# Expert products in three fp16 passes instead of three float32r passes, with scale factors from sums of squares and a new order

## The chip, the cores and the metric

The kernel runs on one core of one Trainium2 chip. The core has TensorE (PE, matrix products into PSUM), VectorE (DVE), ScalarE (ACT), GpSimd (POOL) and SyncE (SP, which here issues the transfers); they run side by side and meet in semaphores. The metric is the time of one execution in device microseconds. Three executions of the kernel before took 581.51 us in the median (581.0 to 586.58).

## The reference, cut to what matters

Causal attention with a memory term over 4 batches, 8 heads, 576 positions and 64 dimensions gives 2304 rows of 512 numbers; these rows go through two dense products with a pointwise function between them, and it is these two that the change rewrites.

```python
scores = where(causal, -1e9, q @ k.T / sqrt(64)); local = softmax(scores) @ v
mem_out = (phi(q) @ M_prev) / (phi(q) @ z_prev + 1e-6)          # phi(x) = x + 1 for x > 0, else exp(x)
x = (g * mem_out + (1 - g) * local)  as (2304, 512)             # g = sigmoid(beta), one per head
h = x @ w_in            # 512 x 2048
out = (h * cos(h)) @ w_out   # 2048 x 512
```

## The kernel before, in words

The 2304 rows are cut into nine chunks of 256: chunk 0 holds the first 64 rows of each batch, chunks 1 and 2 the rest of batch 0, and so on to chunks 7 and 8 of batch 3. The attention of a batch must be done before its chunks can start, so the program is a pipeline: while chunks of one batch are multiplied, the heads of the next batch are computed. The jobs are listed in `prm["jobs"]`: batch 0 in two halves, then one batch each.

A **chunk** begins in `emit_xT`: TensorE turns its rows (L886), ScalarE writes a high part `xh` (L897) and VectorE the rest `xl` (L373). Then come eight **units** of 256 hidden columns each. A unit's first half is `unit1` (PE L914, into `u`): for chunks 1 to 8, 24 matmuls of 256 columns, that is for each of two blocks of 128 hidden columns four blocks of the contraction in three terms (high by high, high by low, low by high) on float32r tiles. `hidden` then makes h cos(h): ScalarE rounds `u` to whole turns (L937), VectorE subtracts (L939), ScalarE takes the sine (L941), VectorE multiplies by `u` (L943); the product is split once more into `gh` (a copy, L363 on ScalarE or L365 on VectorE) and `gl` (a subtraction, L373). The second half is `unit2` (PE L958): 12 matmuls per unit (2 row blocks, 2 blocks of hidden columns, 3 terms), each of 512 columns, into `acc`. `live` holds two units back, so the second half of a unit is issued about two units after its first half. `finish` scales `acc` and stores it. Chunk 0 uses unsplit float32 weights (`weight_val`).

The **weights** come as 64-bit numbers. `load_w` turns a piece of 128 by 512 into float32 in four steps (POOL L476, ACT L479, DVE L481, L486); after chunk 0 has used a piece, `split_w` writes its high part (ACT L504) and its low part (DVE L511), 32 pieces in all.

**Attention heads** go through scores (PE L540), a running minimum (DVE L551), exponentials (ACT L558), a split of the probabilities into two fp16 parts (L363 or L365 for the high one, DVE L570 for the rest), a transposing transfer, and the product with the values (PE L712 in fp16, L703 in float32 for batch 0's first heads), which VectorE adds to the rows (L723). `values` scales the values by a power of two (L627) and splits them into fp16 parts (L365 copy, L373 subtraction).

What sets the **order**: nothing is reordered on the chip except weight loads on TensorE. `Plan.order` runs a list scheduler over all operations with estimated costs (`dve`, `act`, `pool`, `mm`), chooses an engine where an operation allows several (`gl_on` = VectorE or GpSimd, `gh_on`, `hi_on`), and emits the instructions of each engine in the order found. The entries `bdve` and `bact` are added to an operation's finish on VectorE and ScalarE when engines are compared. So the numbers in `prm` decide both order and engine.

Of the kernel before, what the change touches and what calls it, by code (L numbers as in the profile page):

```python
# [292 lines left out]
def kernel(  # L293
# [170 lines left out]
    def load_w(key, src, prio):  # L464
# [24 lines left out]
        w_ready[key] = Pp({"DVE": dve(512)}, end, prio, r=[st, t])  # L489

    def split_w(key, prio, used):
        if len(w_split) >= prm["wide"] and wide:
            ph = pl = wide.pop(0)
        else:
            ph, pl = [(places or last).pop(0) for part in range(2)]

        def high(e):
            if ph == pl:
                both = sb.tile([128, 1024], F32R, tag=ph, name=f"{ph}_both")
                wh[key], wl[key] = both[:, 0:512], both[:, 512:1024]  # L500
            else:
                wh[key] = sb.tile([128, 512], F32R, tag=ph, name=f"{ph}_high")
            if e == "ACT":
                nc.scalar.copy(out=wh[key], in_=wv[key])  # L504
            else:
                eng[e].tensor_scalar(out=wh[key], in0=wv[key], scalar1=1.0, scalar2=1.0, op0=ALU.mult, op1=ALU.mult)
# [665 lines left out]
```

## Time and profile before

| | |
|---|---|
| median of three runs | 581.51 us |
| the profiled execution's span, first to last instruction | 578.5 us |
| median minus span | 3.0 us |
| TensorE busy | 567.5 us (98%) |
| VectorE busy | 402.3 us (70%) |
| ScalarE busy | 407.2 us (70%) |
| GpSimd busy | 160.1 us (28%) |

The profiled execution has no time of its own beside its span; its 578.5 us and what lies around it (3.0 us, if it is a median one) make the 581.5. A busy share is a mean over the whole span. The kernel has two halves: up to about 464 us attention and expert products run together and three engines are loaded; after that only expert products are left. Matmuls are pipelined, so a busy TensorE need not stream without gaps; what one matmul costs in a stream is the distance from start to start, not its duration. On VectorE and ScalarE too an instruction starts some 0.08 us before the record of the one ahead ends.

### The profile page before, as it was taken

The numbers are of one execution on the slowest core, as the hardware profiler recorded it, in microseconds if no ns is written. First come the engines' busy times: TensorE is split into PE (matmuls) and PEld (weight loads), VectorE is DVE, ScalarE is ACT, GpSimd is POOL, SyncE is SP. The second block draws the span as 40 slices with busy tenths as digits, with TensorE's granted clock in tenths as the row PEclk, the third lists the DMA queues.
The fourth block names the chain that finished last, engine by engine and source line by source line (L and its number), as shares of the span: only waits on it lengthen the run. The fifth ranks groups of instructions, "written<-read, shape, count | busy, mean of one in ns | idle before, by whom it ended". The sixth has DMA issues, their size and how long they took to land.

```text
span 578.5 us, 12276 instructions
## 1 busy us (share of the span) xinstructions
PE 567.5 (98%) x4453; PEld 468.6 (81%) x4453; DVE 402.3 (70%) x1292; ACT 407.2 (70%) x872; POOL 160.1 (28%) x159
## 2 busy tenths in 40 slices
PE   8899999999999999999999999999999999999997
PEld 5677657688888788788977988888879999989995
DVE  4999788989989899889758855868698421321320
ACT  4997788898898897769657946968788532433432
POOL 2232330145225213115140311441213112222112
PEclk9999999999999999999999999999999999999999
DMA  8877773696644985485509810727056100000101
GB/s 277 286 228 236 241 231 98 122 200 139 140 97 99 182 160 114 92 168 143 81 0 191 168 31 1 164 76 150 1 103 125 31 1 19 19 0 1 38 0 37
DMA packets 113165, 64.96 MB, mean 112 GB/s; under 512 B 95952, under 2 KB 101584, under 8 KB 113104
## 3 DMA queue, kind: packets, MB, share of 16 engines
q1 hardware_dynamic: 113104, 64.18, 46.7%
q8 instruction: 35, 0.57, 0.4%
q14 instruction: 26, 0.21, 0.1%
HBM read 36.37 MB, written 4.72 MB: 71 GB/s over the span
## 4 chain that ended last, share of the span: by engine, by line
PE 81%; ACT 7%; DMA 5%; DVE 3%; issue 2%; SPq 1%; POOL 0%; ACTq 0%; POOLq 0%; DVEq 0%
PE u L914 32%; PE acc L958 31%; PE S L540 7%; PE pv L712 5%; DMA t<-p 2%; PE pv L703 2%; PE mm L669 2%; ACT s L558 2%; PE mm L886 1%; DMA ws<-in_w_in 1%; DVE p L570 1%; DMA q<-in_qk 1%; SPq L379 1%; ACT p L363 1%; ACT x L689 1%
## 5 line engine op out<-in xcount | busy, mean ns | idle before, releaser
L373 POOL TENSOR_TENSOR gl<-w,gh 128x512 fp32r<-128x512 f32 x64 | 84.7, 1325 | 249.7 <-ACT gh L363 175.2
L914 PE MATMUL u<-xh,weight_high 128*128 128x256 f32 x416 | 119.4, 287 | 1.0 <-DVE w L943 1.0
L914 PE MATMUL u<-xl,weight_high 128*128 128x256 f32 x416 | 115.9, 279 | 0.0
L914 PE MATMUL u<-xh,weight_low 128*128 128x256 f32 x416 | 115.7, 278 | 0.0
L939 DVE SCALAR_TENSOR_TENSOR w<-w,u 128x512 f32<-128x512 int32 x72 | 49.1, 684 | 84.7 <-ACT w L937 68.3
L958 PE MATMUL acc<-weight_high,gh 128*128 128x512 f32 x240 | 97.8, 407 | 0.0
L958 PE MATMUL acc<-weight_low,gh 128*128 128x512 f32 x240 | 94.4, 393 | 0.0
L958 PE MATMUL acc<-weight_high,gl 128*128 128x512 f32 x240 | 94.1, 392 | 0.0
L570 DVE SCALAR_TENSOR_TENSOR p<-s,p 128x64 f16<-128x64 f32 (+1 forms) x224 | 83.1, 414 | 6.2 <-ACT p L363 5.6
L914 PEld LDWEIGHTS u<-xh,weight_high 128*128 128x128 f32 x416 | 78.3, 188 | 6.5 <-issue 2.5
L558 ACT ACTIVATE s<-s,nb 128x448 f32<-128x448 f32 (+3 forms) x128 | 77.6, 610 | 5.9 <-DVE nb L551 5.6
L914 PEld LDWEIGHTS u<-xl,weight_high 128*128 128x128 f32 x416 | 78.3, 188 | 1.4
L914 PEld LDWEIGHTS u<-xh,weight_low 128*128 128x128 f32 x416 | 78.5, 189 | 0.0
L937 ACT ACTIVATE w<-u 128x512 int32<-128x512 f32 x72 | 42.4, 592 | 47.3 <-PE u L914 28.0
L363 ACT ACTIVATE gh<-w 128x512 fp32r<-128x512 f32 x56 | 35.2, 628 | 49.0 <-PE acc L958 40.6
L551 DVE CUSTOM_DVE_ANT_0 s<-S,mask 128x320 f32<-128x320 f32 (+3 forms) x128 | 65.5, 532 | 4.1 <-PE S L540 3.8
L943 DVE TENSOR_TENSOR w<-w,u 128x512 f32<-128x512 f32 x64 | 43.5, 683 | 22.4 <-ACT w L941 22.3
L540 PE MATMUL S<-stq 64*128 64x320 f32 (+4 forms) x320 | 55.6, 455 | 0.0
L941 ACT ACTIVATE w<-w 128x512 f32<-128x512 f32 x72 | 45.0, 629 | 14.8 <-DVE w L939 14.0
L958 PEld LDWEIGHTS acc<-weight_high,gh 128*128 128x128 f32 x240 | 45.1, 188 | 11.2 <-issue 2.7
L958 PEld LDWEIGHTS acc<-weight_low,gh 128*128 128x128 f32 x240 | 45.1, 188 | 10.1
L958 PEld LDWEIGHTS acc<-weight_high,gl 128*128 128x128 f32 x240 | 45.2, 188 | 7.5
(123 smaller groups left out, 1037.0 us busy)
## 6 DMA issues: line engine op xcount, KB each, us to landing
ws<-in_w_in SPq DMA_DIRECT2D x16, 512.0 KB, 5.4
ws<-in_w_out SPq DMA_DIRECT2D x16, 512.0 KB, 4.2
stq<-in_qkp SPq DMA_DIRECT2D x12, 544.0 KB, 4.2
stv<-in_vk SPq DMA_DIRECT2D x16, 320.0 KB, 3.3
out<-w SPq DMA_DIRECT2D x16, 256.0 KB, 2.2
t<-p SPq DMA_TRANSPOSE x112, 3.2
mz<-in_mzp SPq DMA_DIRECT2D x20, 66.0 KB, 2.6
stq<-in_qkp SPq DMA_DIRECT2D x4, 288.0 KB, 3.6
```

Source lines behind the costliest of these rows:

```text
L363: nc.scalar.activation(out=out, in_=in_, func=ACTF.Copy, scale=scale)
L373: lambda e: eng[e].tensor_tensor(out=out, in0=in0, in1=in1, op=ALU.subtract), prio, port=kw.pop('port', True), **kw)
L540: nc.tensor.matmul(out=sv.ap[:, c:c + n], lhsT=pair.ap[p, qs], rhs=pair.ap[p, k0:k0 + n], start=True, stop=True)
L551: return P.op({"DVE": dve(n) + 10}, lambda e: nc.vector.tensor_tensor_reduce(out=st.ap[:, k0:k0 + n], in0=sv.ap[:, c:c + n], in1=mk, scale ...
L558: return P.op({"ACT": act(W, False, 2)}, lambda e: nc.scalar.activation(out=st.ap[:, 0:W], in_=st.ap[:, 0:W], func=ACTF.Exp, scale=-1.0, b ...
L570: Pp({"DVE": dve(n)}, lambda e, c=c, n=n, to=to: nc.vector.scalar_tensor_tensor(out=pt.ap[:, to:to + n], in0=sa[:, c:c + n], scalar=PSCALE ...
L914: nc.tensor.matmul(out=u.ap[:, f, :], lhsT=a[:, cs:cs + 128], rhs=x, start=(n == 0), stop=(n == len(terms) - 1))
L937: P.op({"ACT": act(512)}, lambda e: nc.scalar.activation(out=wi, in_=u.ap, func=ACTF.Copy, bias=0.25), ep, r=[u], w=[w])
L939: P.op({"DVE": dve(512)}, lambda e: nc.vector.scalar_tensor_tensor(out=wv, in0=wi, scalar=0.25, in1=u.ap, op0=ALU.subtract, op1=ALU.subtra ...
L941: P.op({"ACT": act(512, False)}, lambda e: nc.scalar.activation(out=wv, in_=wv, func=ACTF.Sin, scale=-TWO_PI_BELOW), ep, w=[w], table="sin")
L943: P.op({"DVE": dve(512)}, lambda e: nc.vector.tensor_tensor(out=wv if split else views[0], in0=wv, in1=u.ap, op=ALU.mult), ep, r=[u], w=[w ...
L958: nc.tensor.matmul(out=acc[b].ap, lhsT=a, rhs=w, start=(i == 0 and f == 0 and n == 0), stop=(2 * i + f == NF - 1 and n == len(terms) - 1))
```

## The change

Expert products of chunks 1 to 8 take fp16 tiles: `xh`, `xl`, `gh`, `gl` and the split weights become fp16, and a piece of weights has both parts in one tile. So that the parts fit the range of fp16, each is scaled by a power of two: `squares` sums the squares of a piece of weights or of a chunk's rows (ScalarE or VectorE, with a running sum), `powers` adds the sums over partitions with a small matmul and makes a scale from the exponent bits in five small VectorE instructions, and `factors` makes common factors of the eight weight groups once. The scales enter as operands that hold one number per partition: in the copies and subtractions that split, in the rounding and subtraction of `hidden`, in the product with `u` and in `finish`. `xh` and `xl` have two buffers instead of one. Chunk 0 stays as it was.

Lines move by 84 at the end; of the names used here: L914 becomes L985, L958 L1039, L712 L773, L939 L1012, L943 L1016, L373 (subtractions) L381, L365 L373, L627 L688, L511 L568, L570 L631, L551 L612.

```diff
-    group("xh", 1, [128, KD, 256], F32R)
-    group("xl", 1, [128, KD, 256], F32R)
+    group("xh", 2, [128, KD, 256], F16)
+    group("xl", 2, [128, KD, 256], F16)
-    group("gh", 2, [128, 2, 256], F32R)
-    group("gl", 2, [128, 2, 256], F32R)
+    group("gh", 2, [128, 2, 256], F16)
+    group("gl", 2, [128, 2, 256], F16)
...
+        w_norm[key] = squares(prio, wv, key, norms[:, o, j, n:n + 1], after=[w_ready[key]])
+
+    def squares(prio, src, key, to, **kw):
+        def go(e):
+            x = src[key]
...
+                if e == "ACT":
+                    nc.scalar.activation(out=junk[e], in_=x, func=ACTF.Square, accum_out=to)
+                else:
+                    nc.vector.tensor_tensor_reduce(out=junk[e], in0=x, in1=x, scale=1.0, scalar=0.0, op0=ALU.mult,
+                                                   op1=ALU.add, accum_out=to)
...
+    def powers(prio, src, n, q, sc, r=(), a=(), after=()):
+        bank = P.buf("mm")
+        P.op({"PE": 60}, lambda e: nc.tensor.matmul(out=bank.ap[:, 0:n], lhsT=ones.to_broadcast([128, 128]), rhs=src,
+                                                    start=True, stop=True), ...
+        def go(e):
+            nc.vector.tensor_reduce(out=q, in_=bank.ap[:, 0:n], axis=mybir.AxisListType.X, op=ALU.add)
+            nc.vector.tensor_scalar(out=q, in0=q, scalar1=2.0**-100, scalar2=1.0, op0=ALU.max, op1=ALU.mult)
+            nc.vector.tensor_scalar(out=q.bitcast(I32), in0=q.bitcast(I32), scalar1=1, scalar2=0x7F800000, ...)
+            nc.vector.tensor_scalar(out=sc.bitcast(I32), in0=q.bitcast(I32), scalar1=0x7F800000, scalar2=None, ...)
+            nc.vector.tensor_scalar(out=sc, in0=sc, scalar1=2.0**-51, scalar2=None, op0=ALU.mult)
+        return P.op({"DVE": 450}, go, prio, r=[bank], a=a)
...
+                nc.scalar.activation(out=wh[key], in_=wv[key], func=ACTF.Copy, scale=s)
...
-            eng[e].tensor_tensor(out=wl[key], in0=wv[key], in1=wh[key].bitcast(F32), op=ALU.subtract)
+            eng[e].scalar_tensor_tensor(out=wl[key], in0=wv[key], scalar=s, in1=wh[key], op0=ALU.mult, op1=ALU.subtract)
...
+        if len(w_scale) == 8 and not w_fac:
+            w_fac.append(factors(prio))
...
+            P.op({"ACT": act(512, extra=1)}, lambda e: nc.scalar.activation(
+                out=wi, in_=u.ap, func=ACTF.Copy, scale=d, bias=0.25), ep, r=[u, cs], w=[w])
+            P.op({"DVE": dve(512)}, lambda e: nc.vector.scalar_tensor_tensor(
+                out=wv, in0=u.ap, scalar=d, in1=wi, op0=ALU.mult, op1=ALU.subtract), ep, r=[u, cs], w=[w])
+            P.op({"ACT": act(512, False, 1)}, lambda e: nc.scalar.activation(
+                out=wv, in_=wv, func=ACTF.Sin, scale=TWO_PI_BELOW, bias=quarter), ep, w=[w], table="sin", ...)
+            P.op({"DVE": dve(512)}, lambda e: nc.vector.scalar_tensor_tensor(
+                out=wv, in0=wv, scalar=ej, in1=u.ap, op0=ALU.mult, op1=ALU.mult), ep, r=[u], w=[w], after=w_fac)
...
-    "bdve": 1205.026,
-    "bact": 739.67,
+    "bdve": 60.616892,
+    "bact": -403.610341,
+    "sq_on": ('ACT', 'DVE'),
```

Some twenty numbers of `prm` change in all, among them the start `t0` of the chunks and the priorities `xt`, `u2`, `wdt`, `late`; the jobs and the engines that an operation may choose from stay.

Where instructions move. The first place is **GpSimd** behind the last of the weight pieces (`wt`), where the heads of batch 1 and chunk 1 begin: `stv` and `v` are values of heads, `gl` the low part of a unit's hidden numbers. Before:

```order
L476 TENSOR_SCALAR wt_139<-ws_137 128x512
L627 TENSOR_SCALAR stv_67<-stv_67,vs_108 128x640
L365 TENSOR_SCALAR v_72<-stv_67 128x640
L373 TENSOR_TENSOR v_72<-stv_67,v_72 128x640
L627 TENSOR_SCALAR stv_68<-stv_68,vs_109 128x640
L365 TENSOR_SCALAR v_73<-stv_68 128x640
L373 TENSOR_TENSOR v_73<-stv_68,v_73 128x640
L373 TENSOR_TENSOR gl_106<-w_102,gh_104 128x512
L373 TENSOR_TENSOR gl_107<-w_103,gh_105 128x512
```

and now, to the end of GpSimd's work:

```order
L485 TENSOR_SCALAR wt_154<-ws_152 128x512
L688 TENSOR_SCALAR stv_74<-stv_74,vs_123 128x640
L373 TENSOR_SCALAR v_79<-stv_74 128x640
L688 TENSOR_SCALAR stv_75<-stv_75,vs_124 128x640
L688 TENSOR_SCALAR stv_75<-stv_75,vs_125 128x640
L373 TENSOR_SCALAR v_80<-stv_75 128x640
L381 TENSOR_TENSOR v_80<-stv_75,v_80 128x640
```

Before, GpSimd makes all 64 low parts `gl` and all 16 value splits; now it makes 3 of the 64 and 4 of the 16, and the others stand on VectorE.

The second place is **VectorE** around the first two units of chunk 1 (`w` is a unit's working tile, `s`, `S` and `p` belong to the heads). Before:

```order
L939 SCALAR_TENSOR_TENSOR w_103<-w_103,u_129 128x512
L570 SCALAR_TENSOR_TENSOR p_92<-s_83,p_92 128x384
L676 SCALAR_TENSOR_TENSOR r_124<-mm_133,gate 128x4
L943 TENSOR_TENSOR w_102<-w_102,u_128 128x512
L679 RECIPROCAL r_124<-r_124 128x4
L723 SCALAR_TENSOR_TENSOR x_97<-pv_132,sm_121,x_97 128x64
L685 TENSOR_TENSOR x_96<-mm_133,r_124 128x128
L685 TENSOR_TENSOR x_97<-mm_133,r_124 128x128
L570 SCALAR_TENSOR_TENSOR p_90<-s_87,p_90 128x512
L943 TENSOR_TENSOR w_103<-w_103,u_129 128x512
```

and now:

```order
L1016 SCALAR_TENSOR_TENSOR w_111<-w_111,wfac,u_143 128x512
L662 RECIPROCAL sm_133<-sm_133 128x2
L373 TENSOR_SCALAR gh_113<-w_111 128x512
L784 SCALAR_TENSOR_TENSOR x_104<-pv_147,sm_133,x_104 128x64
L784 SCALAR_TENSOR_TENSOR x_103<-pv_147,sm_133,x_103 128x64
L381 TENSOR_TENSOR gl_115<-w_111,gh_113 128x512
L1012 SCALAR_TENSOR_TENSOR w_112<-u_144,cs_117,w_112 128x512
L631 SCALAR_TENSOR_TENSOR p_99<-s_90,p_99 128x384
```

A unit now takes three or four VectorE instructions of 512 columns instead of two (in eight of the 64 units three), between the same work for the heads.

The third place is **VectorE** where chunk 1's rows are split (`xl`). Before:

```order
L570 SCALAR_TENSOR_TENSOR p_93<-s_82,p_93 128x384
L511 TENSOR_TENSOR weight_low<-weight_val,weight_high 128x512
L373 TENSOR_TENSOR xl_101<-mm_133,xh_100 128x4x128
L511 TENSOR_TENSOR wide_both<-weight_val,wide_both 128x512
L511 TENSOR_TENSOR weight_low<-weight_val,weight_high 128x512
```

and now (`wq`, `wsc`, `wfac` and `cs` hold sums and scales):

```order
L528 TENSOR_REDUCE cs_117<-mm_148 128x1
L529 TENSOR_SCALAR cs_117<-cs_117 128x1
L530 TENSOR_SCALAR cs_117<-cs_117 128x1
L532 TENSOR_SCALAR cs_117<-cs_117 128x1
L534 TENSOR_SCALAR cs_117<-cs_117 128x1
L568 SCALAR_TENSOR_TENSOR weight_both<-weight_val,wsc,weight_both 128x512
L942 TENSOR_SCALAR cs_117<-wfac,cs_117 128x5
L373 TENSOR_SCALAR p_97<-s_94 128x576
L568 SCALAR_TENSOR_TENSOR weight_both<-weight_val,wsc,weight_both 128x512
```

Each chunk and each of the eight weight groups has such a chain of small instructions, in which each reads what the one ahead wrote, and the scale stands ahead of what it scales.

## Rows read from the trace of the kernel before

**Rows 1.** The page, busy time and share of each engine.

```profile
PE 567.5 (98%) x4453; PEld 468.6 (81%) x4453; DVE 402.3 (70%) x1292; ACT 407.2 (70%) x872; POOL 160.1 (28%) x159
```

**Rows 2.** The chain in order of time: start us, us, what, records.

```profile
161.08 1.12 PE S L540 x8
...
221.96 1.12 PE pv L712 x38
...
500.66 5.47 PE u L914 x48
...
560.91 13.77 PE acc L958 x60
```

**Rows 3.** Busy time by stretch: PE, PEld, DVE, ACT, POOL, granted clock, DMA.

```profile
0.00:97.00 97.00, 91.33 (x527) 65.03 (x527) 80.70 (x259) 77.48 (x192) 27.82 (x49) 1.00 0.74 238
97.00:160.00 63.00, 62.93 (x527) 48.87 (x527) 57.05 (x177) 56.04 (x112) 21.54 (x18) 1.00 0.69 138
160.00:235.00 75.00, 74.50 (x678) 61.65 (x679) 66.87 (x245) 67.42 (x157) 23.23 (x20) 1.00 0.67 138
235.00:297.00 62.00, 62.00 (x584) 52.17 (x581) 47.19 (x158) 41.94 (x89) 16.62 (x14) 1.00 0.50 99
297.00:579.00 282.00, 276.70 (x2145) 240.93 (x2143) 150.52 (x455) 164.33 (x324) 70.94 (x58) 1.00 0.28 59
```

**Rows 4.** Timeline of ScalarE at the last unit of chunk 3.

```profile
297.00 0.60 ACT L937 ACTIVATE w<-u 128x512 int32<-128x512 f32 x1 [1.46 <-POOL gl L373]
```

**Rows 5.** VectorE's groups by shape: busy us, mean ns, idle before.

```profile
L570 DVE SCALAR_TENSOR_TENSOR p<-s,p 128x512 f16<-128x512 f32 x32 | 25.7, 804 | 0.0
L551 DVE CUSTOM_DVE_ANT_0 s<-S,mask 128x512 f32<-128x512 f32 x32 | 20.9, 683 | 3.8 <-PE S L540 3.8
L551 DVE CUSTOM_DVE_ANT_0 s<-S,mask 128x192 f32<-128x192 f32 x32 | 11.1, 348 | 0.3 <-PE mm L587 0.3
L551 DVE CUSTOM_DVE_ANT_0 s<-S,mask,nb 128x64 f32<-128x64 f32 x32 | 8.9, 277 | 3.6 <-PE S L540 3.3
L624 DVE TENSOR_SCALAR vs<-gate,vs 128x2 f32<-128x2 f32 x16 | 8.7, 546 | 0.2
L365 DVE TENSOR_SCALAR gh<-w 128x512 fp32r<-128x512 f32 x8 | 3.4, 420 | 0.2
```

**Rows 6.** Timeline of VectorE, full instructions back to back.

```profile
149.72 0.68 DVE L570 SCALAR_TENSOR_TENSOR p<-s,p 128x512 f16<-128x512 f32 x1
150.32 0.45 DVE L365 TENSOR_SCALAR p<-s 128x576 f16<-128x576 f32 x1
...
154.18 0.68 DVE L943 TENSOR_TENSOR w<-w,u 128x512 f32<-128x512 f32 x1
154.78 0.68 DVE L939 SCALAR_TENSOR_TENSOR w<-w,u 128x512 f32<-128x512 int32 x1
```

**Rows 7.** Timeline of VectorE, small instructions on the gates.

```profile
9.91 0.17 DVE L427 TENSOR_SCALAR gate<-gate 128x8 f32<-128x8 f32 x1
10.11 0.20 DVE L428 RECIPROCAL gate<-gate 128x8 f32<-128x8 f32 x1
10.35 0.17 DVE L429 TENSOR_SCALAR gate<-gate 128x8 f32<-128x8 f32 x1
```

**Rows 8.** GpSimd's costliest group by shape.

```profile
L373 POOL TENSOR_TENSOR gl<-w,gh 128x512 fp32r<-128x512 f32 x64 | 84.7, 1325 | 249.7 <-ACT gh L363 175.2 <-issue 20.4 <-DVE gh L365 18.3
```

**Rows 9.** Timeline of GpSimd and of VectorE, a small instruction beside `gl`.

```profile
151.15 1.68 POOL L373 TENSOR_TENSOR gl<-w,gh 128x512 fp32r<-128x512 f32 x1 [5.49 <-ACT gh L363]
...
151.81 1.05 DVE L598 TENSOR_SCALAR sm<-sm,vs 128x2 f32<-128x2 f32 x1
...
153.66 0.20 DVE L598 TENSOR_SCALAR sm<-sm,vs 128x2 f32<-128x2 f32 x1
```

**Rows 10.** VectorE's waits up to 297 us: total, times, longest.

```profile
DVE phi L646 <- DMA phi_q<-in_qp: 8.5, 1, 8.5
DVE w L939 <- ACT w L937: 6.4, 6, 2.2
```

More of the change, by code (lines that the diff above doesn't have):

```diff
@@ L489, in load_w @@
         w_ready[key] = Pp({"DVE": dve(512)}, end, prio, r=[st, t])
+        o, j, n = (0, *key[1:]) if key[0] == "i" else (1, *divmod(key[1], 4))
+        w_norm[key] = squares(prio, wv, key, norms[:, o, j, n:n + 1], after=[w_ready[key]])
+    def squares(prio, src, key, to, **kw):
+        def go(e):
+            x = src[key]
+            with nc.allow_low_precision("only the power of two next to the sum is used"):
+                if e == "ACT":
[3 more added lines that the diff above has]
+                                                   op1=ALU.add, accum_out=to)
+        return P.op(some({"ACT": act(512, False, 1), "DVE": dve(512) + 10}, "sq_on"), go, prio, **kw)
@@ L491, in split_w @@
     def split_w(key, prio, used):
[L492 to L495, printed above, removed]
+        place = (places or last).pop(0)
+        o, j = (0, key[1]) if key[0] == "i" else (1, key[1] // 4)
+        s = wsc[:, o, j:j + 1]
         def high(e):
-            if ph == pl:
-                both = sb.tile([128, 1024], F32R, tag=ph, name=f"{ph}_both")
-                wh[key], wl[key] = both[:, 0:512], both[:, 512:1024]
-            else:
[L502 to L506, printed above, removed]
@@ L517, in split_w @@
+        if (o, j) not in w_scale:
+            keys = [("o", 4 * j + n) if o else ("i", j, n) for n in range(4)]
+            w_scale[o, j] = powers(prio, norms[:, o, j, :], 4, wq[:, o, j:j + 1], s, after=[w_norm[k] for k in keys])
+        h = Pp(some({"ACT": act(512, False, 1), "DVE": dve(512, True), "Pool": pool(512)}, "hi_on"), high, prio,
+               after=[w_scale[o, j], *left_by.get(place, list)()])
+        w_ready[key] = Pp({"DVE": dve(512)}, low, prio, after=[h])
         done = [*used, w_ready[key]]
@@ L541, in prod @@
                                      start=True, stop=True)
-        P.op({"PE": 194 + sum(4 * mm(n) for _, _, n, _ in pieces)}, prod, prio, kind="s", r=[pair], w=svs)
+        P.op({"PE": sum(2 * max(200, 93 + n / 1.2) for _, _, n, _ in pieces)}, prod, prio, kind="s", r=[pair], w=svs)
         return svs
@@ L669, in prod @@
                     nc.tensor.matmul(out=mb.ap[p, c], lhsT=a, rhs=b, start=True, stop=True)
-        P.op({"PE": 1.38 * n * nb if whole else 610 + fm * mm(256)}, prod, prio, r=reads, w=[mb],
+        P.op({"PE": 1.7 * n * nb if whole else 610 + fm * mm(256)}, prod, prio, r=reads, w=[mb],
              share=1.0 if whole else (240 + fm * mm(256)) / (610 + fm * mm(256)))
```

135 lines of the change are left out of this document (87 added, 48 removed).

## The prediction

> **What bounds the kernel now.** I read the page's busy shares first: TensorE 98%, VectorE and ScalarE 70% each [rows 1]. That looks like a kernel bound by TensorE alone, so I read the chain of waits for what one matmul costs in a stream, and then the busy time by stretch. The reader is to see two halves. Up to 297.00 us, where ScalarE makes its first piece of the last unit of chunk 3 [rows 4], VectorE is busy 80.7 + 57.05 + 66.87 + 47.19 = 251.8 us, ScalarE 242.9 and TensorE almost throughout, in four stretches [rows 3]: three engines are nearly equally loaded. From 297 us to the end VectorE is busy 150.5 of 282 us and TensorE 276.7: there TensorE alone is the bound. The granted clock is 1.00, 2.4 GHz, in all five. So TensorE's saving counts in full only in the second half; in the first the question is what the change asks of VectorE.
>
> **TensorE.** A float32r matmul of 256 columns takes 5.47/48 = 0.1140 us from start to start, one of 512 columns 13.77/60 = 0.2295, and an fp16 one of 64 columns 1.12/38 = 0.0295 [rows 2]. 64 columns at 2.4 GHz are 0.0267, so an fp16 matmul has 0.0028 over its columns; an estimate for 256 columns is 0.1095 and for 512 0.2161. There are 8 x 8 x 24 = 1536 of the first and 768 of the second: 1536 x 0.0045 + 768 x 0.0134 = 6.9 + 10.3 = 17.2 us less. The 16 small matmuls of `powers` add under 0.1 us each, 1 to 2 us.
>
> **VectorE, up to the same unit.** I counted VectorE's instructions in both orders up to its first piece of chunk 3's last unit (L939, now L1012). A full instruction of 512 columns starts 0.60 us after the one ahead (154.18 to 154.78, and 149.72 to 150.32 with fp16 output and an fp16 operand [rows 6]), so fp16 buys nothing there.
> - `gl`: 20 on VectorE instead of none, 20 x 0.60 = 12.0.
> - Values: nine subtractions of 640 columns (0.60 x 640/512 = 0.73) and seven scalings or copies (0.42 x 640/512, less the 0.08 overlap, = 0.43; `gh`'s 420 ns [rows 5]): 6.6 + 3.0 = 9.6.
> - Squares: nine, priced as the running minimum of 512 columns, 683 ns less 0.08 [rows 5]: 5.4.
> - `powers`: 11 chains of five small instructions. The trace has none, but the gates' chain shows what an instruction costs that needs the one ahead: starts at 9.91, 10.11, 10.35 [rows 7], so 0.20: 11.0, and `factors` 1.2. The plan charges 0.45 a chain, which would be 5; I take 0.20 an instruction, since each reads what the last wrote, and keep 5 as the lower end.
> - `gh`: six more at 0.34, and seven more copies of `p`: 3.
> - Scales per partition: the running minimum takes 683 ns for 512 columns and 348 for 192, so 214 for 64 by that slope; with a per-partition operand (`nb`) it takes 277 [rows 5]. So 0.06 more; 32 weight pieces, 6 of `xl` and 47 in the units: 85 x 0.06 = 5.1. The lower end is nothing.
> - Heads: 24 more of their pieces stand ahead of that unit than before, between 0.20 (277 less 0.08) and 0.60: at 0.33, 8.0.
>
> The sum is 54 to 56, I take 55. Against it stands relief: where VectorE meets GpSimd it is slowed. The same small instruction took 1.05 us beside a `gl` on GpSimd and 0.20 without [rows 9], the low part of `p` 804 ns in the mean against 680 alone, 32 times, which is 4.0 us [rows 5, 6], and L624 546 ns against 200 of a like one, 16 times, 5.5 us [rows 5, 9]. With the smaller differences of the other forms I estimate 25 us in the run and 15 before 297 us; the conversion of the weights stays on GpSimd, so I take back 11 (ends 5 and 15). VectorE then needs 251.8 + 55 - 11 = 296 us there, and it starts only when the first transfer lands, after 8.5 us [rows 10]: 304 without any wait.
>
> **Waits.** Before, VectorE waited 297 - 251.8 - 8.5 = 37 us more in this half, few of them longer than 2 us (`w` on ScalarE 6.4 us in six [rows 10]). An engine that has more to do than the others waits less for them. VectorE now has 304; TensorE's products get shorter, and ScalarE's 242.9 grow by 27 squares, which even at 0.7 us each leave it 40 us below. I take half, 18; the ends are 8 and 37. The unit that ended at 297 is now reached at 322.
>
> **From there to the end** TensorE stays the bound: VectorE's extra work there (41 `gl`, 25 us, and little else) lies beside it, since VectorE has 131 us free; if that cover were gone it would cost those 25. Left of the products are 960 matmuls of 256 columns in both orders, and of 512 columns 540 before and 516 now, as 24 of them moved ahead: 960 x 0.0045 + (540 x 0.2295 - 516 x 0.2161) = 4.3 + 12.4 = 16.7. Ten score matmuls moved ahead too, four of which take 1.12 [rows 2]: 2.8. So 281.5 - 19.5 = 262 us. 322 + 262 = 584 us of span. Around the span lie 3.0 us against the median of 581.5, so **587 us**: 5.5 over the median, 0.9% more. The transfers are the same in number and size but for the order; the tail is covered by its units: GpSimd's 1325 ns for `gl` [rows 8] becomes 0.60 on VectorE, ahead of a second half that is issued two units later, so it gives nothing.
>
> **The rivals.** Times within 1% cannot be told from no change by a measurement of this kernel, that is 575.7 to 587.3.
> - *Forecast: VectorE takes over as the bound up to chunk 3 and gives back what TensorE gains later.* With waits between 12 and 26, 581 to 595. Chance 0.44.
> - *TensorE stays the bound throughout and the saving arrives whole:* 581.5 - 17.2 + 1 = 565 (558 to 571, the lower end if the change of kind between fp16 and float32r matmuls costs something now). For that VectorE must reach the unit by 300 us, with no waits left or far more relief than I take. A mechanism: GpSimd's work blocks VectorE for most of its length, so that 20 `gl` of 1.33 us [rows 8] and the values that leave give back some 40 us instead of 11; then 322 - 29 = 293, and TensorE decides. Rows 9 speak for the mechanism, the mean of 804 against 680 ns against its size. Chance 0.22.
> - The Trainium skill, *GPSIMD Engine Reference*, Specifications, says that GpSimd shares its SBUF interfaces with VectorE, with contention for VectorE instructions that have two SBUF inputs or run in a two-port mode. The trace agrees in kind, 1.05 against 0.20 us [rows 9]; taken as blocking for GpSimd's whole length, it would give the 565 of this rival, by the trace's mean the forecast.
> - *Cheap small work:* the chains overlap (6 less), scales cost nothing (5 less): 322 - 11 = 311, so 576 (571 to 581). Chance 0.18.
> - *Coupling as before:* VectorE waits as long as it did, 37 us. The single PSUM buffer `mm` speaks for it: the 16 sums pass through it between turning rows and memory products, so TensorE stands behind VectorE's chains and VectorE behind TensorE's sums. 341 + 262 + 3 = 606 (596 to 609). Chance 0.14.
> - *The fp16 passes do not go faster than the float32r ones*, as fp16 has a weight load of its own per matmul: 19.5 shrinks to some 8.5, 598. The fp16 stream of 0.0295 us with a load for each matmul speaks against it [rows 2]. Chance 0.02.
>
> **How the numbers follow.** The time is the forecast's, 587. Faster by over 1%: the second case but for a little and a third of the cheap one, 0.28. Slower by over 1%: a good half of the forecast, the coupling and the fp16 case, 0.40. Within 1% 0.32. The range goes from 562 to 603: below it lies half of the full-saving case (0.11), above it most of the coupling case (0.08). The forecast's own range is 581 to 595.
>
> **What would show it.** In the profile after, L985 must stream at 0.110 and L1039 at 0.216 us, and GpSimd be busy some 45 us. VectorE must be busy about 290 us or more of the time to the first piece of chunk 3's last unit, with that piece at 310 to 335 us instead of 297, and the five instructions of a chain stand 0.2 us apart. From there to the end some 262 us. If that piece comes at 300 us or earlier, the forecast is wrong in VectorE's sum or in the waits; if it comes at 320 and the end is still below 575, the remainder was not bound by TensorE alone and the new order fills it better.

## The result and the profile after

The changed kernel takes 587.17 us in the median of 20 runs (582.53 to 589.39), the one before 580.63 (578.5 to 586.58): the ratio is 1.0107, with a 95% interval from 1.0083 to 1.0132. It is slower by 1.1%, at the edge of what such a measurement can tell; the forecast was 587.0. The profiled executions have spans of 587.5 and 578.5 us. The one after took 589.2 us, 2.0 over its median, at a mean granted clock of 0.981; the 20 executions after range from 0.979 to 0.991.

The page after, busy time of each engine and the granted clock in 40 slices of 14.7 us:

```profile
PE 555.6 (95%) x4469; PEld 380.0 (65%) x4469; DVE 466.2 (79%) x1504; ACT 436.8 (74%) x944; POOL 45.5 (8%) x66
...
PEclk9978999999999999997999999999899999999999
```

Against [rows 1], TensorE is busy 12 us less in a span that is 9 us longer, and has gone from 11 us of idle time to 32. VectorE has 64 us more, GpSimd 115 less. The clock, 1.00 in every stretch of [rows 3], now falls below 0.9 in four of the 40 slices.

The chain of waits after, start us, us, what, records:

```profile
302.81 5.24 PE u L985 x48
...
411.79 6.91 PE u L985 x48
...
573.29 10.37 PE acc L1039 x48
```

At the full clock a matmul of 256 columns takes 5.24/48 = 0.1092 us and one of 512 columns 10.37/48 = 0.2160, where [rows 2] had 0.1140 and 0.2295. So TensorE's products became shorter by what was forecast. The run at 411.79 shows the same 48 matmuls taking 1.67 us more in a stretch of lower clock.

ScalarE's first piece of chunk 3's last unit, which stood at 297.00 us [rows 4] and is called the marker from here on, in the timeline after:

```profile
319.18 0.67 ACT L1010 ACTIVATE w<-u,cs 128x512 int32<-128x512 f32 x1
```

Busy time by stretch after, cut at the same units as [rows 3] (PE, PEld, DVE, ACT, POOL, granted clock, DMA):

```profile
0.00:107.90 107.90, 96.65 (x546) 69.60 (x547) 90.48 (x304) 90.15 (x241) 28.82 (x50) 0.95 0.66 217
107.90:175.10 67.20, 62.34 (x549) 41.17 (x548) 66.61 (x215) 61.17 (x121) 2.33 (x3) 1.00 0.60 124
175.10:248.70 73.60, 69.96 (x650) 47.00 (x647) 68.85 (x258) 62.75 (x150) 8.45 (x8) 1.00 0.65 135
248.70:319.20 70.50, 66.64 (x611) 45.94 (x610) 62.00 (x226) 57.63 (x127) 1.96 (x2) 0.95 0.60 114
319.20:587.50 268.30, 260.01 (x2126) 176.30 (x2122) 178.26 (x506) 165.06 (x312) 3.97 (x3) 0.99 0.26 57
```

All of the loss, 22.2 us, arises up to the marker; 13.2 of it come back behind it (281.5 us became 268.3). In the second stretch VectorE is busy 66.61 of 67.20 us and TensorE 62.34, where before TensorE was busy 62.93 of 63.00. The bound has changed hands, as the forecast said. But the last row is not one stretch of TensorE's. The same view, cut finer:

```profile
319.00:376.00 57.00, 55.19 (x501) 37.97 (x498) 51.45 (x168) 43.57 (x93) 0.00 (x0) 1.00 0.55 112
376.00:437.00 61.00, 58.90 (x548) 40.83 (x547) 49.46 (x169) 47.84 (x96) 3.97 (x3) 0.97 0.39 84
437.00:489.00 52.00, 51.47 (x451) 35.78 (x449) 37.61 (x110) 34.01 (x63) 0.00 (x0) 1.00 0.19 42
489.00:531.70 42.70, 42.70 (x301) 29.17 (x299) 19.74 (x33) 18.62 (x29) 0.00 (x0) 1.00 0.04 13
```

Up to 437 us VectorE is still busy 81 to 90% of the time, and TensorE idle about 2 us in each of the two stretches. From there on TensorE is busy with hardly a gap.

VectorE's groups by shape after (busy us, mean ns, idle before), to be held against [rows 5]:

```profile
L1012 DVE SCALAR_TENSOR_TENSOR w<-u,cs,w 128x512 f32<-128x512 f32 x64 | 47.7, 746 | 26.5 <-ACT w L1010 26.2
L381 DVE TENSOR_TENSOR gl<-w,gh 128x512 f16<-128x512 f32 x61 | 42.0, 690 | 27.2 <-ACT gh L371 26.9
L631 DVE SCALAR_TENSOR_TENSOR p<-s,p 128x512 f16<-128x512 f32 x32 | 21.8, 682 | 0.0
L685 DVE TENSOR_SCALAR vs<-gate,vs 128x2 f32<-128x2 f32 x16 | 3.5, 221 | 0.0
```

`gl` is new there. `p` of 512 columns fell from 804 to 682 ns and the small instruction on `vs` from 546 to 221 while GpSimd is quiet. That GpSimd is the reason shows in a run below that only moves its work, in the old order: there they go from 779 to 684 and from 517 to 225. What an instruction loses depends on what it meets, though: with the work back on GpSimd in the new order `vs` takes 493 ns again and `p` of 512 columns 678. The turning of a unit, `w` on L1012, takes 746 ns with its scale per partition.

One chain of `powers` in the timeline of VectorE after:

```profile
46.41 0.14 DVE L528 TENSOR_REDUCE wq<-mm 128x1 f32<-128x4 f32 x1
46.59 0.15 DVE L529 TENSOR_SCALAR wq<-wq 128x1 f32<-128x1 f32 x1
46.78 0.15 DVE L530 TENSOR_SCALAR wq<-wq 128x1 int32<-128x1 int32 x1
46.97 0.15 DVE L532 TENSOR_SCALAR wsc<-wq 128x1 int32<-128x1 int32 x1
47.15 0.15 DVE L534 TENSOR_SCALAR wsc<-wsc 128x1 f32<-128x1 f32 x1
47.23 0.27 DVE L784 SCALAR_TENSOR_TENSOR x<-pv,sm,x 128x64 f32<-128x64 f32 x1
```

They start 0.18 to 0.19 us apart; L784, which needs none of them, starts 0.08 behind the last one.

TensorE's waits after: engine and tile, what it waited for, total us, times, longest:

```profile
PE u L985 <- DVE w L1016: 6.2, 8, 1.5
PE mm L954 <- DVE xl L968: 2.8, 2, 2.4
PE pv L773 <- DMA t<-p: 2.7, 2, 2.1
PE mm L954 <- ACT s L960: 2.5, 1, 2.5
```

Of the 27.4 us in that view 16.6 end with an instruction of VectorE, above all `w` of a unit and `xl`, the rows of a new chunk. Behind the marker, of the same view, only these count for more than 0.3 us:

```profile
PE pv L773 <- DMA t<-p: 2.1, 1, 2.1
PE u L985 <- DVE w L1016: 1.9, 3, 0.7
```

### The profile page after: what moved, and what is told of

Its sections match the earlier page's. It is cut to its first block, busy times and chain, and to the rows that moved or that the text cites. A ratio compares the mean times of both kernels' runs of the same rounds, so it can differ in the third digit from the quotient of the medians.

```text
span 587.5 us, 12444 instructions
## 1 busy us (share of the span) xinstructions
PE 555.6 (95%) x4469; PEld 380.0 (65%) x4469; DVE 466.2 (79%) x1504; ACT 436.8 (74%) x944; POOL 45.5 (8%) x66
## 4 chain that ended last, share of the span: by engine, by line
PE 57%; DVE 25%; DMA 8%; ACT 4%; issue 4%; SPq 0%; POOL 0%; DVEq 0%; ACTq 0%
PE u L985 24%; PE acc L1039 22%; DMA t<-p 6%; DVE p L631 4%; DVE s L612 4%; PE S L601 4%; PE pv L773 3%; DVE w L1016 2%; DVE weight_both L568 2%; PE pv L764 2%; DVE x L784 1%; DVE w L1012 1%; PE mm L730 1%; DVE gl L381 1%; DVE weight_val L495 1%
## 5 line engine op out<-in xcount | busy, mean ns | idle before, releaser
L985 PE MATMUL u<-xh,weight_both 128*128 128x256 f16 x1024 | 182.1, 276 | 6.2 <-DVE w L1016 6.2
L985 PEld LDWEIGHTS <-weight_both 128*128 128x128 f16 x1536 | 149.9, 99 | 37.6 <-issue 13.3
L1039 PE MATMUL acc<-weight_both,gh 128*128 128x512 f16 x512 | 164.8, 379 | 0.0
L985 PE MATMUL u<-xl,weight_both 128*128 128x256 f16 x512 | 141.1, 276 | 0.4 <-DVE xl L968 0.4
L1039 PE MATMUL acc<-weight_both,gl 128*128 128x512 f16 x256 | 97.1, 379 | 0.0
L1039 PEld LDWEIGHTS <-gh 128*128 128x128 f16 x512 | 50.0, 98 | 56.5 <-issue 3.3
L619 ACT ACTIVATE s<-s,nb 128x320 f32<-128x320 f32 (+3 forms) x128 | 77.4, 607 | 3.3 <-DVE nb L612 3.0
L631 DVE SCALAR_TENSOR_TENSOR p<-s,p 128x64 f16<-128x64 f32 (+3 forms) x224 | 72.6, 365 | 3.7 <-ACT p L371 3.4
L612 DVE CUSTOM_DVE_ANT_0 s<-S,mask 128x320 f32<-128x320 f32 (+3 forms) x128 | 65.8, 534 | 3.9 <-PE S L601 2.2
L1012 DVE SCALAR_TENSOR_TENSOR w<-u,cs,w 128x512 f32<-128x512 f32 x64 | 47.7, 746 | 26.5 <-ACT w L1010 26.2
L381 DVE TENSOR_TENSOR gl<-w,gh 128x512 f16<-128x512 f32 x61 | 42.0, 690 | 27.2 <-ACT gh L371 26.9
L601 PE MATMUL S<-stq 64*128 64x448 f32 (+4 forms) x320 | 58.9, 462 | 2.3 <-DMA stq<-in_qkp 1.5
L1016 DVE SCALAR_TENSOR_TENSOR w<-w,wfac,u 128x512 f32<-128x512 f32 x64 | 47.4, 744 | 12.6 <-ACT w L1014 12.2
L773 PEld LDWEIGHTS <-t 128*128 128x128 f16 x1112 | 36.7, 98 | 10.5 <-issue 4.0
L773 PE MATMUL pv<-v,t 128*128 128x64 f16 x1112 | 38.3, 193 | 4.4 <-DMA t<-p 2.7
L1039 PEld LDWEIGHTS <-gl 128*128 128x128 f16 x256 | 25.0, 98 | 21.6 <-DVE gl L381 0.2
L985 PE MATMUL u<-s,weight_val 128*128 128x256 f32 x128 | 34.0, 417 | 0.6 <-DVE t L1027 0.6
```

The costliest lines, as they stand in the source:

```text
L381: lambda e: eng[e].tensor_tensor(out=out, in0=in0, in1=in1, op=ALU.subtract), prio, port=kw.pop('port', True), **kw)
L601: nc.tensor.matmul(out=sv.ap[:, c:c + n], lhsT=pair.ap[p, qs], rhs=pair.ap[p, k0:k0 + n], start=True, stop=True)
L612: return P.op({"DVE": dve(n) + 10}, lambda e: nc.vector.tensor_tensor_reduce(out=st.ap[:, k0:k0 + n], in0=sv.ap[:, c:c + n], in1=mk, scale ...
L619: return P.op({"ACT": act(W, False, 2)}, lambda e: nc.scalar.activation(out=st.ap[:, 0:W], in_=st.ap[:, 0:W], func=ACTF.Exp, scale=-1.0, b ...
L631: Pp({"DVE": dve(n)}, lambda e, c=c, n=n, to=to: nc.vector.scalar_tensor_tensor(out=pt.ap[:, to:to + n], in0=sa[:, c:c + n], scalar=PSCALE ...
L773: nc.tensor.matmul(out=pv.ap[:, 64 * i:64 * i + 64], lhsT=got[r].ap[:, block, :], rhs=vals.ap[:, part, h % 2, 64 * j:64 * j + 64], start=( ...
```

## The experiments

The question is where 19 us of shorter products went. The theory (A): VectorE's added load ahead of chunk 4 is passed on to the end. Its rivals: the order and the loss of GpSimd cost it, whatever VectorE has to do (B); or the scaling's waits do, through `mm` and the chains (C). Each ratio is to the kernel before, run on the same chip.

| kernel | median us | ratio, 95% interval | marker us |
|---|---|---|---|
| before | 580.63 | 1 | 297.0 |
| after | 587.17 | 1.0107 (1.0083 to 1.0132) | 319.2 |
| fp16 alone, old order | 561.01 | 0.9656 (0.9598 to 0.9714) | 290.5 |
| after, work back on GpSimd | 589.5 | 1.0134 (1.0062 to 1.0206) | 317.0 |
| after, no sums | 577.61 | 0.9939 (0.9899 to 0.9979) | 311.7 |
| after, no sums and no scales | 573.67 | 0.9866 (0.9828 to 0.9904) | 306.2 |
| fp16 alone, old order, `gl` and values on VectorE | 568.62 | 0.9813 (0.9769 to 0.9857) | 294.8 |
| after's code, numbers of before | 582.17 | 1.0036 (1.0017 to 1.0055) | 306.1 |
| after, 24 instructions more in chunks 1 to 3 | 599.13 | 1.0366 (1.0305 to 1.0427) | 327.7 |
| after, the same in chunks 4 to 6 | 597.98 | 1.0291 (1.0242 to 1.0340) | 318.6 |
| after, the same in the last 24 units | 588.54 | 1.0132 (1.0065 to 1.0200) | 318.5 |
| after, corrected costs in the planner | 583.26 | 1.0047 (1.0010 to 1.0085) | 316.7 |
| the same, numbers of before | 582.55 | 1.0045 (1.0012 to 1.0078) | 308.0 |
| fp16 alone, old order, 24 instructions more in chunks 1 to 3 | 573.3 | 0.9872 (0.9809 to 0.9936) | 301.9 |

**fp16 alone in the old order.** The kernel before with fp16 tiles for `xh`, `xl`, `gh`, `gl` and the split weights. It leaves out all scaling, so it relies on the range of these inputs.

```diff
-    group("xh", 1, [128, KD, 256], F32R)
+    group("xh", 1, [128, KD, 256], F16)
...
-            eng[e].tensor_tensor(out=wl[key], in0=wv[key], in1=wh[key].bitcast(F32), op=ALU.subtract)
+            eng[e].tensor_tensor(out=wl[key], in0=wv[key], in1=wh[key], op=ALU.subtract)
```

> The kernel before with one thing changed: the tiles of the expert products of chunks 1 to 8 are fp16 instead of float32r. No scaling, no sums of squares, the old numbers and so the old order and engines. Theory A (VectorE decides up to chunk 3, TensorE after it): the 960 and 540 matmuls behind chunk 3's last unit give 4.3 + 7.2 = 11.5 us, the 576 and 228 ahead of it up to 5.6 more, as far as TensorE binds there: 563 to 570 us, with the first piece of that unit at 291 to 297 us. Rival B (the shorter matmuls need the new order to be worth anything, since the engines wait for each other): 577 to 581 us.

561.0 us, 19.4 less than before and 2 below the range of theory A; the marker, at 290.5, is just ahead of its range too. Its page, and its busy time up to the marker and behind it:

```profile
PE 543.4 (97%) x4453; PEld 372.7 (67%) x4453; DVE 399.2 (72%) x1292; ACT 406.7 (73%) x872; POOL 151.3 (27%) x159
```

```profile
0.00:290.50 290.50, 281.26 (x2310) 194.91 (x2311) 250.32 (x837) 242.71 (x549) 85.64 (x101) 1.00 0.68 166
290.50:558.20 267.70, 262.11 (x2145) 177.75 (x2143) 148.91 (x455) 164.02 (x324) 65.70 (x58) 1.00 0.30 63
```

VectorE has the 250 us up to the marker that it had before (251.8), and the marker comes 6.5 us earlier, the rest of the gain, 13.8, behind it. So the saving of the three passes is real and arrives whole where VectorE's load stays. This is the fastest kernel of all, and its four executions had a granted clock of 0.997 to 1.000.

**Work back on GpSimd.** The order of after, with `gl`, the value subtractions and scalings issued on GpSimd.

```diff
-            o.fn(o.eng)
+            o.fn("Pool" if o.back else o.eng)
```

> The changed kernel in its own order, but all 64 low parts gl and all value subtractions and scalings are issued on GpSimd, as before the change. Theory A with contention: VectorE loses 20 x 0.61 + 9 x 0.74 + 6 x 0.47 = 21.7 us up to chunk 3's last unit, and the slowing by GpSimd that had gone comes back, some 15 to 19 us: 582 to 590 us, no change. Rival C (contention is small, the move to VectorE is what cost): 566 to 572 us. Rival D (GpSimd blocks VectorE for its whole length, and gl is late by 0.6 us each time): 595 us or more.

```profile
PE 554.8 (95%) x4469; PEld 379.1 (65%) x4469; DVE 438.0 (75%) x1420; ACT 437.3 (75%) x944; POOL 145.1 (25%) x150
```

No change, 589.5, as expected with contention. 84 instructions left VectorE: 61 `gl` at 0.61 us from start to start (690 ns less the 0.08 overlap), 12 subtractions at 0.74 and 11 scalings at 0.47, 51 us; but VectorE is busy only 28.2 us less. The other 23 us came back, most of them as slower instructions beside GpSimd (the 16 on `vs` alone by 16 x 0.272 = 4.4 us). In this order the choice of engine is neutral, so the loss of GpSimd is not the cause by itself.

**Without the sums, and without the scales too.** The first leaves out the squares, the small matmuls, the chains and the factors and takes constants as scales; the second also takes the plain operations of before, so no scaling is left.

```diff
+        nc.gpsimd.memset(wsc, 1.0)
+        nc.gpsimd.memset(wfac, 1.0)
...
-        P.op({"PE": 60}, lambda e: nc.tensor.matmul(out=bank.ap[:, 0:n], lhsT=ones.to_broadcast([128, 128]), rhs=src,
+        P.op({"PE": 60}, lambda e: None,
```

> The changed kernel in its own order without the sums of squares, the small matmuls, the chains of five, the factors and the scaling of the factors per chunk; the scales are constants (1, and 2 pi at the end), written once at the start. Left out is the choice of the powers of two. Theory A: VectorE has 9 x 0.61 + 11 x 0.93 + 1.2 = 17 us less up to chunk 3's last unit, which comes at 302 to 307 us instead of 319, and the time is 570 to 575 us. Rival E (the engines hold each other, through the one PSUM buffer mm and the waits, and VectorE's sum is not what decides): 580 to 586 us.

```diff
-                out=wv, in0=u.ap, scalar=d, in1=wi, op0=ALU.mult, op1=ALU.subtract), ep, r=[u, cs], w=[w])
+                out=wv, in0=wi, scalar=0.25, in1=u.ap, op0=ALU.subtract, op1=ALU.subtract), ep, r=[u, cs], w=[w])
```

> As e3_no_sums, and the scales per partition are gone too: plain copies, subtractions and products as in the kernel before, in the changed kernel's order. Left out is all scaling. Theory A: 85 instructions of VectorE up to chunk 3's last unit are 0.06 us shorter, 5 us, and the time is 565 to 570 us, 4 to 6 below e3_no_sums. Rival E: as e3_no_sums within 2 us. Beside e1_fp16_old_order it shows what the new order and the new engines are worth without scaling: within 1% of it under theory A.

The sums are worth 9.6 us and the scales 3.9 more (the two intervals just touch, so the second size is weak); the marker moves 7.5 and 5.5. Both expectations were missed: theory A asked for 570 to 575 us without the sums, and for 565 to 570 and no more than 1% above fp16 alone without the scales too, where it is 2.3%. VectorE's busy time fell by 19.6 us in the run without the sums, and part of that turned into waits. How much of the 9.6 us is VectorE's time and how much the waits of theory C is not separated here. What is left, 573.7, stands 12.7 us above fp16 alone in the old order, with the same operations: that is the price of the new order and of the engines chosen in it, the granted clock included (0.988 to 0.997 here).

**Old order, `gl` and values on VectorE.** The same move the other way round, in the fp16 kernel with the old order.

```diff
-            o.fn(o.eng)
+            o.fn("DVE" if o.back else o.eng)
```

> e1_fp16_old_order with one thing moved: all 64 gl and the value subtractions and scalings are issued on VectorE, in the old order's places. If the choice of engine is what cost the changed kernel 12.7 us between e1 (561.0) and e4_no_scales (573.7), this takes 570 to 575 us. If it is the order of the program, and engine choice is worth nothing either way, as e2_back_on_gpsimd (589.5 against 587.2) says, it takes 559 to 564 us.

```profile
PE 544.7 (96%) x4453; PEld 372.8 (66%) x4453; DVE 437.2 (77%) x1388; ACT 406.4 (72%) x872; POOL 38.0 (7%) x63
```

`p` of 512 columns in fp16 alone, and then here:

```profile
L570 DVE SCALAR_TENSOR_TENSOR p<-s,p 128x512 f16<-128x512 f32 x32 | 24.9, 779 | 0.0
L571 DVE SCALAR_TENSOR_TENSOR p<-s,p 128x512 f16<-128x512 f32 x32 | 21.9, 684 | 0.0
```

568.6, 7.6 us more than fp16 alone, between the two expectations. VectorE is busy 38.0 us more for 96 instructions that need 58; again about 20 us return as relief from GpSimd. So of the 12.7 us some 7.6 go with the work that VectorE took over, and about 5 stay with the order, if the two may be added; that the opposite move changed nothing in the new order puts it in doubt.

**The numbers of before.** The code of after with the old `prm`, `gl` all on GpSimd, planned anew.

```diff
-    "bdve": 60.616892,
-    "bact": -403.610341,
+    "bdve": 1205.026,
+    "bact": 739.67,
```

> The changed kernel's code, all scaling included, with the numbers of the kernel before (order and engines planned from them, gl and values on GpSimd). Theory A': the new numbers cost some 12 us and the scaling up to 13.5, and in the old kind of order VectorE has more waits to take the scaling up: 566 to 575 us, faster than both. Rival: the old numbers do not fit the new work (eight chains ahead of chunk 1, one more pass over the weights), and it takes 580 us or more.

582.2: 5 us better than after, 21 over fp16 alone, and what the rival expected, not theory A'. Here the scaling, with the plan made for it and the granted clock that comes with it (0.982 to 0.996), costs those 21 us, though `gl` stays on GpSimd and VectorE has 431.8 us of busy time instead of after's 466.2.

**Load added in three places.** One VectorE product of 512 columns more in each of 24 units, 24 x 0.60 = 14.4 us: in chunks 1 to 3, then 4 to 6, then in the last 24 units.

```diff
+                if 0 <= nth < 24:
+                    nc.vector.tensor_tensor(out=junk["DVE"], in0=w.ap, in1=w.ap, op=ALU.mult)
```

> The changed kernel with one more VectorE instruction of 512 columns (0.60 us, its result is not used) in each of the 24 units of chunks 1 to 3, 14.4 us in all. Theory A (VectorE decides up to chunk 3): 598 to 603 us, with chunk 3's last unit 10 to 15 us later than 319.2. Rival (waits between the engines decide, VectorE has 24 us of them to give): 587 to 592 us.

> The same 24 instructions in the units of chunks 4 to 6. Theory A (TensorE decides there, VectorE has 92 us free): 587 to 591 us. Rival (VectorE decides there too, through the heads of batch 3): 596 us or more.

> As e8_load_later, with the 24 extra VectorE instructions (14.4 us) in the last 24 units (chunks 6 to 8), most of which come after the last head. After e8 (598.0) the point from which TensorE alone decides is open. If it is the last head (some 480 us): 586 to 590 us. If VectorE decides even there, through the second halves that wait for gl: 594 us or more.

12.0, 10.8 and 1.4 us, the last within the noise of the two medians. The first shows the forecast's mechanism: what VectorE gets ahead of chunk 4 is passed on; the marker moved by 8.5 us, less than the 10 to 15 expected. The second went against theory A: in chunks 4 to 6 it is passed on too. Its busy time there and the wait that took it in:

```profile
320.00:378.00 58.00, 54.81 (x487) 37.66 (x486) 53.88 (x169) 42.81 (x91) 0.00 (x0) 0.97 0.51 101
378.00:440.00 62.00, 57.72 (x526) 39.46 (x525) 53.11 (x173) 46.87 (x95) 4.49 (x3) 0.97 0.39 82
```

```profile
PE u L985 <- DVE w L1023: 11.6, 11, 3.4
```

TensorE's wait for the turned `w` is 11.6 us instead of 6.2. VectorE fills 86 to 93% of these stretches, and takes in little more: the last units of chunks 4, 5 and 6 fall behind those of after by 3.4, 3.6 and 2.4 us more each, for 4.8 us of load. In the third run chunk 6 still takes 2.1 us longer for its 4.8 us (54.1 from the last unit of chunk 5 to its own, against 52.0), chunks 7 and 8 together 0.9 us for 9.6. Only behind the heads does an added instruction cost next to nothing.

**Corrected costs in the planner.** The plan charges 450 ns for a chain of `powers` and nothing for a scale; the chain shown above takes 0.9 us (46.41 to 47.30), and a scale 62 ns. I put 930 and 62, and doubled the cost of `factors` and of its product per chunk in like manner. Planned anew with these, with the new numbers and with the old ones.

```diff
-        return P.op({"DVE": 450}, go, prio, r=[bank], a=a)
+        return P.op({"DVE": 930}, go, prio, r=[bank], a=a)
...
-            P.op({"DVE": dve(512)}, lambda e: nc.vector.scalar_tensor_tensor(
+            P.op({"DVE": dve(512) + 62}, lambda e: nc.vector.scalar_tensor_tensor(
```

> The changed kernel with the planner's VectorE costs set to what the trace shows: 0.93 us instead of 0.45 for a chain of five, 1.2 instead of 0.6 for the factors, 0.06 more for each instruction with a scale per partition. Order and engines are planned anew with the changed kernel's numbers. If the too small costs are why the new order loads VectorE ahead of chunk 4: 575 to 582 us. If not (the numbers fit only the order they were found with): 584 us or more.

> The same corrected costs with the numbers of the kernel before, that is e6_old_numbers (582.2) planned with the measured costs. If costs matter: 572 to 579 us. If not: 580 to 585 us.

583.3 and 582.6: 4 us better than after with the new numbers, nothing with the old ones. The first lies between its two expectations, the second in that of the rival, that costs do not matter. As the times stand, the price that the plan did not know explains a small part only. But in the median both kernels ran at the lowest granted clocks of all, 0.978 and 0.976 against 0.984 in after, so a gain in the order may be hidden in them; no run separates it.

**Load in the old order.** The fp16 kernel in the old order, with the same 24 instructions in chunks 1 to 3.

```diff
+            if split and nth < 24:
+                nc.vector.tensor_tensor(out=junk, in0=w.ap, in1=w.ap, op=ALU.mult)
```

> e1_fp16_old_order (561.0) with the same 24 extra VectorE instructions (14.4 us) in the units of chunks 1 to 3. In e1 VectorE, ScalarE and TensorE are about equally loaded there and VectorE waits some 30 us of 290. If equal engines pass a load on as the changed order does (12 of 14.4 in e7): 570 to 575 us. If those waits take it up: 562 to 567 us.

573.3, that is 12.3 of 14.4 us passed on, as expected: with the short products VectorE decides up to chunk 3 in the old order as well. fp16 alone has no slack left there; it only asks for nothing more.

Between the runs, the span splits into TensorE's busy and idle time, both from the page, and the granted clock:

| kernel | span | TensorE busy | idle | mean clock |
|---|---|---|---|---|
| before | 578.5 | 567.5 | 11.0 | 0.999 |
| fp16 alone | 558.2 | 543.4 | 14.8 | 1.000 |
| the same, load in chunks 1 to 3 | 571.2 | 546.7 | 24.5 | 1.000 |
| no sums, no scales | 571.9 | 550.0 | 21.9 | 0.988 |
| after | 587.5 | 555.6 | 31.9 | 0.981 |
| corrected costs, old numbers | 579.8 | 556.1 | 23.7 | 0.976 |

Against fp16 alone, after has 17.1 us more idle time and 12.2 more busy time with the same products and sixteen small matmuls more. The clock's shortfall, 0.019 x 587.5 = 11 us, is of the size of the latter.

Does a lower clock cost time, or only fill waits for VectorE? Two runs have after's instructions in a stretch, but not its dip. Behind the marker, from the last unit of chunk 4 to that of chunk 5, first after, then the run with load in the last 24 units, where the load starts later:

```profile
376.00:437.10 61.10, 59.00 (x552) 40.93 (x551) 49.46 (x169) 47.85 (x97) 3.97 (x3) 0.97 0.39 84
375.30:434.80 59.50, 57.40 (x551) 39.96 (x550) 49.03 (x169) 47.46 (x97) 3.97 (x3) 1.00 0.40 86
```

The dip goes with 1.6 us of TensorE's busy time and with 1.6 us of time: there it costs in full. (From the last unit of chunk 1 to that of chunk 2, at a clock of 1.00 in all three runs, they take 73.1 to 73.8 us; so much is noise.) Ahead of the marker, from the last unit of chunk 2 to that of chunk 3, the run with load in chunks 4 to 6 has no dip where after has a clock of 0.95 in 70.5 us:

```profile
249.10:318.50 69.40, 64.76 (x609) 44.36 (x610) 62.14 (x226) 57.55 (x126) 1.97 (x2) 1.00 0.65 118
```

TensorE is busy 1.9 us less there, and the stretch is 1.1 us shorter: of a shortfall of 0.05 x 70.5 = 3.5 us, about a third arrives where VectorE is busy for 62 of those 70.5 us.

The executions say the same of the whole. Those of the kernel before that were run beside the experiments have spans of 576.4 to 578.2 us at a granted clock of 1.000 (15 of them) and of 584.1 to 585.3 at 0.985 (7); after has 580.8 and 581.4 at 0.991 and 586.1 to 587.7 at 0.979 to 0.981. So 0.01 of clock goes with about 5 us in both. At 0.985 the two kernels are nearly alike: 584.6 to 587.0 in six executions after. The kernel before has 0.996 or more in 43 of 50, after never more than 0.991. So far as these executions show, most of the 1.1% between the two goes with the clock; that they lose it in the same places is not shown. What went ahead of the dips is taken up at the end.

## Why the prediction was right

**TensorE's term** of 17.2 us held: 0.1092 and 0.2160 us a matmul against the estimates 0.1095 and 0.2161, and 19.4 us in the kernel with fp16 alone. The rival that fp16 brings a weight load per matmul had no ground: [rows 1] has as many loads as matmuls before.

**VectorE takes over up to chunk 3** held. It was to be busy 296 us there and was 90.48 + 66.61 + 68.85 + 62.00 = 287.9. The prices that could be read were right within a few hundredths (a scale 746 - 684 = 0.062 us against 0.06, a link of a chain 0.19 against 0.20). The 8 us that it was busy less are not relief. Up to the marker, before and after:

```profile
L624 DVE TENSOR_SCALAR vs<-gate,vs 128x2 f32<-128x2 f32 x10 | 6.3, 635 | 0.1
L685 DVE TENSOR_SCALAR vs<-gate,vs 128x2 f32<-128x2 f32 x11 | 2.4, 220 | 0.0
```

That is 10 x 0.415 = 4.2 us of relief on `vs`. The low parts of `p`, taken shape by shape in the same way, give 5.2, the conversion `wt` (494 ns, now 436, 32 times) 1.9, and the whole comes to some 11 us, an estimate, as forecast. So the added work took about 47 us of busy time instead of 55; which term was how much too large I have not followed. In the whole run the two moves above put the relief at 20 and 23, where I had estimated 25.

**The waits** were 319.2 - 287.9 - 7.2 = 24 us, where 7.2 is VectorE's first wait for a transfer, and not 18. So two errors, 8 us less of work and 6 more of waits, nearly cancel, and the marker stood at 319.2 where 322 was forecast; that is luck. The added load shows the mechanism (12.0 of 14.4 us passed on), taking off the sums the opposite way (9.6 us). From fp16 alone to after the runs add up: 9.6 us for the sums, 3.9 for the scales and 12.7 for the new order and its engines make the 26.2 between 561.0 and 587.2, more than the 19.4 that the shorter products gave.

**The step that failed** is "VectorE's extra work there lies beside it, since VectorE has 131 us free". The 131 us were an average over 282 us. The stretches after show VectorE 81 to 90% busy up to 437 us and under half busy behind 489; the 24 instructions in chunks 4 to 6 cost 10.8 us, in the last units 1.4. So the remainder took 268.3 us instead of 262. TensorE was to be busy 276.7 - 19.5 = 257.2 us of it and idle 5.3, as before; it was busy 260.0 and idle 8.3. Of the 2.8 of busy time 1.67 stand in the chain's piece at 411.79, where the clock is lower. Of the waits behind the marker, 1.9 us are for `w` on VectorE and 2.1 are one wait for a transposing transfer, ahead of that piece. A forecast that cut the second half at the end of the heads would have seen VectorE's part; the clock it could not have read from the rows of before.

**The number itself** fits in part by luck. The forecast takes the clock at 1.00 throughout. The executions after have 0.984 in the median, and by the 5 us per 0.01 above that is worth some 7 us, an estimate; at the full clock the forecast would have been about that much too high. On the other side stand the 6 us by which the remainder was too short. And what lies around the span is 589.2 - 587.5 = 1.7 us, not the 3.0 of the sum.

**The rivals.** That TensorE stays the bound is out: the marker came at 319, not 293. GpSimd's work does slow VectorE, but by 23 us for some 100 us of it (145.1 - 45.5), which is far from blocking for its whole length. By the Trainium skill, *GPSIMD Engine Reference*, Specifications, the two engines contend for their SBUF interfaces when an instruction of VectorE has two SBUF inputs; the trace agrees in kind, 779 against 684 ns for `p`, which reads two tiles, where only GpSimd's work was moved. The cheap small work is out by the price of the chains; the coupling as before is out in its size, though TensorE's waits on `mm` for `xl` and its neighbours (2.8 and 2.5 us) are the waits that it spoke of.

**What stays open** is the order's own part, some 5 us between 568.6 and 573.7, of which the clock may be about half (0.991 and 0.997 in the median, by the estimate above), and how much of after's time would come back if its dips could be avoided in this order.

## What to carry to other kernels

When the bound engine is relieved, ask first what the next engine has free in each stretch, not in the run: here 19 us saved on TensorE were worth 19 us only while VectorE got nothing more to do, and sums, scales and a new order took 26 us back. Bound a stretch by where its load changes, at the end of the heads here, and test cover by adding a known load to it. Moving work between VectorE and GpSimd changed VectorE's busy time by 55 and 66% of what the instructions say, in the two moves made here; the rest came back as contention. And read the granted clock of every execution beside its time: here most of the difference of 1.1% went with it.
